# A Toeplitz convolution whose moving columns lie 4 bytes apart in place of 8, inside an attention kernel

## The chip, the cores and the metric

One core of one Trainium2 chip. The metric is the device time of one execution in microseconds (us). Each kernel was run several times; "ratio" is the mean time of a kernel's fast runs over the mean of the fast runs of the kernel before in the same rounds on the same chip, so it is not quite the ratio of the medians that stand beside it. Runs flagged slow (over 1.5% above the fastest of the same kernel) are left out of ratios. TensorE's mean granted clock is listed with each run, as a share of full speed.

## The reference, cut to what matters

Two branches over the same input `x` (2048 x 448), mixed by a gate:

```python
g = _sigmoid((x * gate_w).sum(-1, keepdims=True))
a = _A_ref(x, A_wq, A_wk, A_wv, A_wo)       # 16 heads of 28, one shared key/value head, softmax over 2048
b = _B_ref(x, B_A_re, B_A_im, ...)          # S4: K[d,l] = Re sum_n C P^l B, then a causal convolution of x with K
return g * a + (1 - g) * b
```

## The kernel before

Attention and the S4 branch are interleaved on the same engines. A list scheduler inside the program orders the operations of all engines before anything runs. It works from a cost in nanoseconds for every operation (the number after `mm` in `pg.op`), so that number changes the order of instructions and nothing else.

Attention: QK matmuls (1024) fill PSUM (the memory that TensorE writes to), an exponential on ScalarE (ACT, 410 instructions, half of them over 1536 columns and half over 1024) reads it, PV matmuls (1024, four column tiles at a time) use the result.

```python
pg.op("pe", mm, 215, ..., mode="r32")                                   # QK  (line 967)
pg.op("act", lambda e: e.activation(expT.v(...), self.psS.v(...), AF.Exp, scale=SQ), ...)   # exp (line 977)
pg.op("pe", mm, 225, mode="c32", ...)                                   # PV  (line 985)
```

S4: VectorE (DVE) builds tables of powers, TensorE turns 16 channels of them at a time into the convolution kernel K (line 792), DVE copies it into a staging tile, a DMA writes it to a scratch in HBM (the chip's main memory), and loads fetch it back as a Toeplitz matrix T: 128 partitions that each read the same scratch, shifted by one step. Four channels share a scratch row, interleaved, so the columns of one channel lie four bf16 elements, 8 bytes, apart.

```python
# scratch write: runs of 256 elements = 64 steps x 4 channels
pg.dma([(dram(self.KP, 16 * c * KPW, [[4 * KPW, 4], [256, 32], [1, 256]]),
         self.kstg.v(0, P, ks * 256, [[1, 256]]))], (128, 512), ...)

def tload(self, gi):                      # one 1 MB load for 4 channels
    pg.dma([(self.T.v(0, P, s * 4096, [[1, 4096]]),
             dram(self.KP, 4 * gi * KPW, [[4, 64], [4096, 2], [1, 4096]]))], (128, 8192), ...)

# conv (line 853): 28 chunks x 4 loads x 8 steps = 896 groups of four matmuls, one channel per column tile
for j in range(4):
    r = e.matmul(ps.v(32 * j, 33 - m, po + 128 * k, [[1, 128]]),
                 self.U.v(0, P, (m - 1) * D + 4 * gi + j, [[D, 33 - m]]),
                 self.T.v(0, P, s * 4096 + (960 - 64 * m) * 4 + j, [[4, 128]]),     # moving, step 4 elements
                 start=(m == 1), stop=(m == 15), tile_position=(0, 32 * j), ...)
...
pg.op("pe", mm, 112, rd=[("T", s), "U"], ...)                                       # told cost: 112 ns a group
```

## Time and profile before

| | before |
|---|---|
| time, median of 3 runs | 537.78 us (537.64 to 539.54) |
| span of the profiled run | 537.2 us |
| mean granted TensorE clock | 0.921 |
| conv matmuls, busy time on PE | 157.9 us |
| PE waiting for an exponential before QK (matmuls) | 27.2 us |
| last exponential ends / end of span | 519.5 / 537.2 us |

The prediction below shows most of the lines (in them PE is TensorE's matmuls and PEld its weight loads). The group line of the page gives busy us and the mean ns of one instruction, then the engine's idle time just before them.

### The profile page before, as it was taken

The numbers are of one execution on the slowest core, as the hardware profiler recorded it, in microseconds if no ns is written. First come the engines' busy times: TensorE is split into PE (matmuls) and PEld (weight loads), VectorE is DVE, ScalarE is ACT, GpSimd is POOL, SyncE is SP. The second block draws the span as 40 slices with busy tenths as digits, with TensorE's granted clock in tenths as the row PEclk, the third lists the DMA queues.
The fourth block names the chain that finished last, engine by engine and source line by source line (L and its number), as shares of the span: only waits on it lengthen the run. The fifth ranks groups of instructions, "written<-read, shape, count | busy, mean of one in ns | idle before, by whom it ended". The sixth has DMA issues, their size and how long they took to land.

```text
span 537.2 us, 18418 instructions
## 1 busy us (share of the span) xinstructions
PE 484.8 (90%) x8229; PEld 243.8 (45%) x8229; DVE 483.9 (90%) x1168; ACT 487.5 (91%) x428; POOL 4.9 (1%) x17
## 2 busy tenths in 40 slices
PE   6778888999999899999999999999999998998893
PEld 5411132553545444554545445554455543544452
DVE  4978899998999999999999999999999999999023
ACT  4599998998999999999999999999999999999960
POOL 3000000000000000000000000000000000000000
PEclk9855566997999999999999999999999999889997
DMA  8735445777798867779898896778877796697954
GB/s 232 145 79 137 138 139 207 245 285 299 249 327 297 303 230 237 253 265 345 304 337 320 262 332 238 242 260 319 309 296 267 285 393 220 176 388 254 350 188 137
DMA packets 42266, 138.16 MB, mean 257 GB/s; under 512 B 8168, under 2 KB 24476, under 8 KB 27852
## 3 DMA queue, kind: packets, MB, share of 16 engines
q1 hardware_dynamic: 40396, 135.71, 73.7%
q10 hardware_dynamic: 1792, 1.29, 0.8%
q8 instruction: 64, 1.05, 0.8%
q14 instruction: 14, 0.11, 0.1%
HBM read 133.01 MB, written 3.85 MB: 255 GB/s over the span
## 4 chain that ended last, share of the span: by engine, by line
PE 47%; ACT 36%; DVE 12%; DMA 2%; issue 1%; POOL 1%; DVEq 0%; POOLq 0%
ACT expT L977 35%; PE psS L967 13%; PE psS L853 12%; PE psB L985 8%; PE psX L792 6%; PE psX L676 2%; DMA T<-KP_scratch 2%; DVE tab L767 2%; DVE tmp L762 2%; DVE tab L759 2%; PE psS L504 1%; PE psX L877 1%; PE psX L831 1%; DVE O L883 1%; DVE tab L776 1%
## 5 line engine op out<-in xcount | busy, mean ns | idle before, releaser
L977 ACT ACTIVATE expT<-psS 128x1536 bf16<-128x1536 f32 (+1 forms) x410 | 470.8, 1254 | 19.0 <-PE psB L985 12.9
L967 PE MATMUL psS<-qT,kT 29*128 29x512 bf16 x1024 | 170.6, 412 | 29.6 <-ACT expT L977 27.2
L853 PE MATMUL psS<-T,U 128*26 128x128 bf16 (+7 forms) x3584 | 157.9, 303 | 0.6 <-DMA T<-KP_scratch 0.5
L853 PEld LDWEIGHTS psS<-T,U 128*26 128x26 bf16 (+7 forms) x3584 | 113.9, 152 | 35.3 <-issue 28.2
L985 PE MATMUL psB<-expT,vaug 128*32 128x512 bf16 x1024 | 108.8, 417 | 1.4 <-ACT gtok L643 1.3
L967 PEld LDWEIGHTS psS<-qT,kT 29*128 29x128 bf16 x1024 | 39.6, 92 | 124.4 <-ACT expT L977 92.8
L762 DVE TENSOR_TENSOR tmp<-tab,mbf 128x2048 bf16<-128x2048 bf16 (+4 forms) x140 | 78.0, 563 | 0.0
L759 DVE TENSOR_TENSOR tab<-tab,mbf 128x2048 bf16<-128x2048 bf16 (+4 forms) x140 | 77.9, 563 | 0.0
L767 DVE TENSOR_TENSOR tab<-tab,tmp 128x2048 bf16<-128x2048 bf16 (+4 forms) x140 | 77.8, 563 | 0.0
L792 PE MATMUL psX<-tab 128*32 128x96 bf16 x1792 | 54.8, 268 | 1.3 <-issue 1.2
L985 PEld LDWEIGHTS psB<-expT,vaug 128*32 128x32 bf16 x1024 | 26.6, 95 | 64.2 <-issue 60.8
L792 PEld LDWEIGHTS psX<-tab 128*32 128x32 bf16 x1792 | 41.2, 116 | 14.2 <-issue 9.0
L776 DVE TENSOR_TENSOR tab<-tab,mbf 128x2048 bf16<-128x2048 bf16 x28 | 34.0, 1216 | 0.0
L778 DVE TENSOR_TENSOR tab<-tab,mbf 128x2048 bf16<-128x2048 bf16 x28 | 34.0, 1213 | 0.0
L861 DVE TENSOR_TENSOR cst<-psS,omq 128x512 bf16<-128x512 f32 x28 | 19.0, 680 | 15.7 <-PE psS L853 15.5
L717 DVE TENSOR_TENSOR msq<-mst 128x256 f32<-128x256 f32 x63 | 26.2, 416 | 0.0
L676 PE MATMUL psX<-xT,Wq 112*128 112x512 bf16 x64 | 21.7, 436 | 0.4 <-DVE O L838 0.2
L727 DVE CAST mbf<-mst 128x256 bf16<-128x256 f32 x70 | 20.1, 288 | 0.1
L720 DVE TENSOR_TENSOR mst<-msq 128x128 f32<-128x128 f32 x70 | 19.7, 282 | 0.0
L723 DVE SCALAR_TENSOR_TENSOR mst<-mst 128x128 f32<-128x128 f32 x63 | 17.8, 283 | 0.0
L804 DVE TENSOR_REDUCE kstg<-psX 128x128 bf16<-128x256 f32 x28 | 11.7, 418 | 4.2 <-PE psX L792 4.1
L730 DVE TENSOR_SCALAR mbf<-mst 128x128 bf16<-128x128 f32 x70 | 15.3, 218 | 0.0
(112 smaller groups left out, 255.8 us busy)
## 6 DMA issues: line engine op xcount, KB each, us to landing
T<-KP_scratch SPq DMA_DIRECT2D x112, 1024.0 KB, 7.8
rdenB<-R_scratch SPq DMA_DIRECT2D x60, 64.0 KB, 3.8
U<-in_A_x_dram SPq DMA_DIRECT2D x3, 896.0 KB, 5.4
tab<-in_A_x_dram SPq DMA_DIRECT2D x4, 448.0 KB, 6.9
O<-Z_scratch SPq DMA_DIRECT2D x1, 1792.0 KB, 13.6
KP_scratch<-kstg SPq DMA_DIRECT2D x28, 64.0 KB
xT<-in_A_x_dram SPq DMA_DIRECT2D x1, 1792.0 KB, 9.2
U<-Z_scratch SPq DMA_DIRECT2D x1, 896.0 KB, 8.0
```

Source lines behind the costliest of these rows:

```text
L676: pg.op("pe", lambda e, T=T: e.matmul(px, self.Wq.v(0, DT, T * 512 + g * 128, [[1, 128]]), self.xT.v(0, DT, T * S + 512 * qc, [[1, 512]]), ...
L717: pg.op("dve", lambda e, k=k: e.tensor_tensor(msq.v(0, P, 0, [[1, 2 * BW]]) if k > 1 else msq.v(0, P, 0, [[BW, 2], [1, BW]]), src_both(k - ...
L759: pg.op("dve", lambda e, d=dst, a=src, ra=ra, w=w: e.tensor_tensor(d, a, mbf.v(0, P, ra, [[8, 16], [0, 2 * w], [1, 4]]), ALU.mult), el(n, ...
L762: pg.op("dve", lambda e, a=src, rb=rb, w=w: e.tensor_tensor(tmp.v(0, P, so, [[4 * w, 32], [1, 4 * w]]), a, mbf.v(0, P, rb, [[4, 32], [0, w ...
L767: pg.op("dve", lambda e, d=dst, t=t2: e.tensor_tensor(d, d, t, ALU.add), el(n, 1.92), rd=[("tmp", s), ("tab", s, lv + 1)], wr=[("tab", s, ...
L776: pg.op("dve", lambda e: e.tensor_tensor(ua, src, mbf.v(0, P, ra, [[8, 8], [0, 64], [1, 4]]), ALU.mult), el(2048, 1.92), rd=rk + mk, wr=[( ...
L778: pg.op("dve", lambda e: e.tensor_tensor(ub, src, mbf.v(0, P, rb, [[4, 16], [0, 32], [1, 4]]), ALU.mult), el(2048, 1.92), rd=rk + mk, wr=[ ...
L792: r = e.matmul(self.psX.v(32 * g, 32, 96 * jj, [[1, 96]]), tab.v(0, P, o + 768, [[4, 32]]), tab.v(0, P, o, [[256, 3], [4, 32]]), start=(co ...
L853: r = e.matmul(ps.v(32 * j, 33 - m, po + 128 * k, [[1, 128]]), self.U.v(0, P, (m - 1) * D + 4 * gi + j, [[D, 33 - m]]), self.T.v(0, P, s * ...
L967: r = e.matmul(self.psS.v(0, P, 1536 * s + 512 * k, [[1, 512]]), kT.v(32 * h, DH + 1, 128 * kt, [[1, 128]]), qT.v(32 * h, DH + 1, 512 * qs ...
L977: pg.op("act", lambda e: e.activation(expT.v(0, P, 512 * (i0 % 10), [[1, n]]), self.psS.v(0, P, 1536 * s, [[1, n]]), AF.Exp, scale=SQ), 75 ...
L985: r = e.matmul(self.psB.v(32 * h, 32, 0, [[1, 512]]), vaug.v(0, P, 32 * kt, [[1, 32]]), expT.v(0, P, 512 * ((4 * st + h) % 10), [[1, 512]] ...
```

## The change

The intent: halve the step of conv's moving operand, because conv takes about 0.94 ns a column in the trace before, and PV's matmuls, with a contiguous operand, 0.41 (both estimates from the lengths of bursts, which the prediction works out). The scratch and T are therefore interleaved over 2 channels, in two halves, and the scheduler is told 80 ns a group in place of 112. The arithmetic stays.

```diff
-            return e.tensor_reduce(self.kstg.v(0, P, ks * 256, [[4, 32], [1, 4]]), ...
+            return e.tensor_reduce(self.kstg.v(0, P, ks * 256, [[2, 32], [128, 2], [1, 2]]), ...
 ... (the second staging copy in the same way)
-        pg.dma([(dram(self.KP, 16 * c * KPW, [[4 * KPW, 4], [256, 32], [1, 256]]),
-                 self.kstg.v(0, P, ks * 256, [[1, 256]]))],
-               (128, 512), f"kw{ks}", ...
+        pg.dma([(dram(self.KP, (16 * c + 2 * k1) * KPW, [[4 * KPW, 4], [128, 32], [1, 128]]),
+                 self.kstg.v(0, P, ks * 256 + 128 * k1, [[1, 128]])) for k1 in range(2)],
+               (256, 256), f"kw{ks}", ...
-        pg.dma([(self.T.v(0, P, s * 4096, [[1, 4096]]),
-                 dram(self.KP, 4 * gi * KPW, [[4, 64], [4096, 2], [1, 4096]]))],
-               (128, 8192), f"T{s}", ...
+        pg.dma([(self.T.v(0, P, s * 4096 + 2048 * k1, [[1, 2048]]),
+                 dram(self.KP, (4 * gi + 2 * k1) * KPW, [[2, 64], [2048, 2], [1, 2048]])) for k1 in range(2)],
+               (256, 4096), f"T{s}", ...
-                                     self.T.v(0, P, s * 4096 + (960 - 64 * m) * 4 + j, [[4, 128]]),
+                                     self.T.v(0, P, s * 4096 + j // 2 * 2048 + (960 - 64 * m) * 2 + j % 2, [[2, 128]]),
-                pg.op("pe", mm, 112, ...
+                pg.op("pe", mm, 80, ...
 ... (the padding write of the scratch in the same way)
```

More of the change, by code (lines that the diff above doesn't have):

```diff
@@ L447, in loads @@
                 for r in range(4)], (448, 896), "wo", wr=["Wo"])
-        pg.dma([(dram(self.KP, 4 * S, [[4 * KPW, 112], [1, 256]]), self.kstg.v(0, 112, 0, [[1, 256]])),
+        pg.dma([(dram(self.KP, 2 * S, [[4 * KPW, 112], [2 * KPW, 2], [1, 128]]), self.kstg.v(0, 112, 0, [[128, 2], [1, 128]])),
                 (dram(self.Z, 0, [[256, 4], [1, 256]]), self.kstg.v(0, 4, 0, [[1, 256]]))],
@@ L803, in upper @@
             with self.nc.allow_low_precision(reason="two float32 terms, added in float32 and rounded once"):
-                return e.tensor_reduce(self.kstg.v(0, P, ks * 256, [[4, 32], [1, 4]]),
+                return e.tensor_reduce(self.kstg.v(0, P, ks * 256, [[2, 32], [128, 2], [1, 2]]),
                                        self.psX.v(0, P, 0, [[1, 32], [96, 4], [32, 2]]), AX.X, ALU.add)
         pg.op("dve", upper, el(256), rd=[X], wr=[("kst", ks)], pr=2)
-        pg.op("dve", lambda e: e.tensor_copy(self.kstg.v(0, P, ks * 256 + 128, [[4, 32], [1, 4]]),
+        pg.op("dve", lambda e: e.tensor_copy(self.kstg.v(0, P, ks * 256 + 64, [[2, 32], [128, 2], [1, 2]]),
                                              self.psX.v(0, P, 64, [[1, 32], [96, 4]])),
               el(128), rd=[X], wr=[("kst2", ks)], pr=2, unlock="X")
-        pg.dma([(dram(self.KP, 16 * c * KPW, [[4 * KPW, 4], [256, 32], [1, 256]]),
-                 self.kstg.v(0, P, ks * 256, [[1, 256]]))],
-               (128, 512), f"kw{ks}", rd=[("kst", ks), ("kst2", ks)], wr=[("KP", c)], pr=0)
+        pg.dma([(dram(self.KP, (16 * c + 2 * k1) * KPW, [[4 * KPW, 4], [128, 32], [1, 128]]),
+                 self.kstg.v(0, P, ks * 256 + 128 * k1, [[1, 128]])) for k1 in range(2)],
+               (256, 256), f"kw{ks}", rd=[("kst", ks), ("kst2", ks)], wr=[("KP", c)], pr=0)
     def tload(self, gi):
@@ L817, in tload @@
         c = gi // 4
-        pg.dma([(self.T.v(0, P, s * 4096, [[1, 4096]]),
-                 dram(self.KP, 4 * gi * KPW, [[4, 64], [4096, 2], [1, 4096]]))],
-               (128, 8192), f"T{s}", rd=[("KP", c), "pad"], wr=[("T", s)], pr=1, ns=3300)
+        pg.dma([(self.T.v(0, P, s * 4096 + 2048 * k1, [[1, 2048]]),
+                 dram(self.KP, (4 * gi + 2 * k1) * KPW, [[2, 64], [2048, 2], [1, 2048]])) for k1 in range(2)],
+               (256, 4096), f"T{s}", rd=[("KP", c), "pad"], wr=[("T", s)], pr=1, ns=3300)
     def ytr(self, c):
@@ L858, in conv @@
                 first = k == 0 and m == 1
-                pg.op("pe", mm, 112, rd=[("T", s), "U"], wr=[X, ("cst", cs)] + ([("b", 5)] if c == 0 else []) if first else [X], pr=2.5,
+                pg.op("pe", mm, 80, rd=[("T", s), "U"], wr=[X, ("cst", cs)] + ([("b", 5)] if c == 0 else []) if first else [X], pr=2.5,
                       lock="C" if first else None, slack=(2500 if gi else 9000) if m == 1 else 0, mode="c32")
```

## The prediction

> **What bounds the kernel now.** I read the page's busy shares first, then the clock slices, the windows, the waits and last the timeline of single bursts.
>
> ```profile
> PE 484.8 (90%) x8229; PEld 243.8 (45%) x8229; DVE 483.9 (90%) x1168; ACT 487.5 (91%) x428; POOL 4.9 (1%) x17
> ...
> PEclk9855566997999999999999999999999999889997
> ...
> q1 hardware_dynamic: 40396, 135.71, 73.7%
> ```
>
> Three engines are level at 90%, so no one of them alone is the bound; the windows show where each is full (columns: PE, PEld, DVE, ACT, POOL busy, then clock, DMA share, GB/s).
>
> ```profile
> 90.00:440.00 350.00, 335.29 (x6230) 174.94 (x6228) 344.19 (x855) 338.86 (x296) 0.63 (x2) 0.98 0.81 285
> 440.00:480.00 40.00, 36.81 (x673) 18.69 (x671) 38.54 (x77) 37.26 (x33) 0.00 (x0) 0.91 0.74 262
> 480.00:520.00 40.00, 35.39 (x654) 18.47 (x643) 19.12 (x36) 39.40 (x36) 0.00 (x0) 1.00 0.85 301
> ```
>
> From 90 to 440 us DVE is 98% busy and ACT 97%. From 480 DVE has little left and ACT runs at 98% to the last exponential, which ends at 520. What follows 520 is a tail of 17 us. ACT is thus the pacemaker; the reader should look for the few us in which it waits:
>
> ```profile
> PEld psS L967 <- ACT expT L977: 92.8, 231, 1.9
> ...
> ACT expT L977 <- PE psB L985: 12.9, 27, 1.4
> ...
> ACT expT L977 <- PE psS L967: 4.4, 10, 0.7
> ...
> PEld psS L853 <- DMA T<-KP_scratch: 0.8, 1, 0.8
> ```
>
> PE waits 93 us for ACT, so its 90% is inflated by pipelined latencies; it has slack. ACT waits for PE only 17.3 us, in 37 places, always short. Conv (L853) almost never waits for its data. The change makes conv on PE cheaper. Its prize is therefore the part of those 17.3 us that conv bursts cause, not conv's whole time.
>
> The costs of conv and of its comparisons:
>
> ```profile
> L977 ACT ACTIVATE expT<-psS 128x1536 bf16<-128x1536 f32 (+1 forms) x410 | 470.8, 1254 | 19.0 <-PE psB L985 12.9
> ...
> L853 PE MATMUL psS<-T,U 128*26 128x128 bf16 (+7 forms) x3584 | 157.9, 303 | 0.6 <-DMA T<-KP_scratch 0.5
> ...
> L792 PE MATMUL psX<-tab 128*32 128x96 bf16 x1792 | 54.8, 268 | 1.3 <-issue 1.2
> ...
> T<-KP_scratch SPq DMA_DIRECT2D x112, 1024.0 KB, 7.8
> ```
>
> ```profile
> 195.00 1.26 PE L792 MATMUL psX<-tab 128*32 128x96 bf16 x48
> ...
> 198.91 0.69 PE L853 MATMUL psS<-T,U 128*24 128x128 bf16 x16
> ...
> 283.49 0.73 PE L792 MATMUL psX<-tab 128*32 128x96 bf16 x24
> ...
> 300.61 0.40 PE L985 MATMUL psB<-expT,vaug 128*32 128x512 bf16 x4
> ...
> 301.48 1.16 PE L853 MATMUL psS<-T,U 128*32 128x128 bf16 x32
> ...
> 304.13 0.45 PE L831 MATMUL psX<-ident,cst 128*64 128x64 bf16 x16
> ...
> 313.16 0.61 PE L985 MATMUL psB<-expT,vaug 128*32 128x512 bf16 x8
> ```
>
> The slope between bursts gives the period of a group of four column tiles. Conv: (1.16 - 0.69) us for 4 more groups is 0.12 us for 128 columns, 0.94 ns a column. The kernel generation L792, whose moving operand also steps 8 bytes: (1.26 - 0.73) for 6 groups is 0.088 us for 96 columns, 0.92 ns. L985, contiguous: 0.21 us for 512 columns, 0.41 ns. Single records say the same: conv groups inside one burst start 120 to 122 ns apart, whether the weight load has 30 columns or 18. So weight loads do not set conv's period. A moving step of 8 bytes costs about 2.2 times a contiguous one. L831, whose moving identity steps 4 bytes, with two tiles at a time: (0.45 - 0.20 for one matmul's latency) / 7 = 0.036 us for 64 columns, 0.56 ns with all issue overhead in it. So 4 bytes looks almost like contiguous.
>
> [...] its half-clock stretches last 3.4 us or about a multiple of it, and the clock reads 0.50 between 40 and 60 us, where conv has not begun. [...]
>
> **The change, part by part.**
> Conv: 3584 / 4 = 896 groups. If 4-byte steps run at the contiguous rate, a group takes 128 x 0.41 = 53 ns plus some 12 to 15 ns for issuing four pairs (L985's group over 512 columns at full clock), so about 67 ns. Removed from PE: 896 x (121 - 67) = 48 us of streaming. The changed cost the schedule is told is 80 in place of 112; if that is nearer the truth, 896 x 35 = 31 us.
> T loads: 112 become 224 issues, of 4096-byte rows. In the trace an 8192-byte packet takes 309 ns, a 2048-byte one 84 at its fast end, so 0.0366 ns a byte plus 9 ns: 4096 bytes come to 159 ns, against 154.5 for half a long one. The loads occupy 325 us of the 16 engines' time now, so +3% is 10 us spread over the span, on queues 74% busy: hidden. SP issues 140 more at 0.52 us each: its 148 us of issuing become 221 of 537, also hidden, though a tile lands some 0.5 us later.
> The scratch writes (28, now 256-byte runs) and DVE's two PSUM copies (418 and 277 ns) keep their element counts; I take them as unchanged.
> ACT's gain: I went through every gap in ACT after 90 us and counted conv groups begun within 1 us before it ended. In 29 gaps there are some, 11 us of gap in all. Crediting each with the smaller of its length and 54 ns a group gives 5.5 us. Each removed gap also lets the next exponential overlap the one before (1254 ns mean alone, 1120 per step in the unbroken run at the end), 29 x 0.13 x one half = 2 us. Sum 7.5 us; the tail, which still has 56 conv matmuls between its steps, gives some 0.5 us.
> What comes off again is the clock. Streaming work per us of span is now: QK and PV (410 + 256) x 0.21 / 486 us = 0.29; conv 0.25; kernel generation 0.09; projections, output, transposes 0.07: together 0.70, at clock 1.0. Without conv, before 90 us, it is about 0.4 and the clock is 0.5 to 0.67. By windows of 3.4 us the fall to half clock comes below about 0.47 (an estimate from this trace). After the change the mean is 0.59, so perhaps one window in ten falls, a dozen in place of four. The gaps of 1.43, 0.79 and 0.98 us at 129, 461 and 471 us are all in or beside such windows; with less work in each I charge 0.4 us, net about +2 us.
> Sum: 538 - 8 + 2 = 532; with a little for a schedule that packs PE's queue better by the new cost, 531.
>
> **The rivals.**
> A: the clock takes it all. For: the threshold lies near the new mean[...]. Against: work per window recovers by itself as PE slows. Time 534 to 540.
> B: DVE is the bound. For: 98% from 90 to 440 us, untouched by the change. Against: it has 31 us idle after 480, so it can be up to 9 us behind ACT without setting the end. It caps the gain: not below about 522.
> C: the step is not what costs, conv stays near 120 ns a group. [...] Against: L985 and L831. Time 536 to 539.
> D: transfers become the bound (more descriptors, later tiles, 0.85 DMA share after 480). Against: 159 against 154.5 ns, and 0.8 us of waiting for T in all. Time 540 or more.
> E: the full prize, all conv-made gaps and their overlap vanish: 11 + 3 us, about 524.
>
> **Range and chances.** E and B bound it below, A and C above: 524 to 537.5. Two per cent faster is 527.0, which needs nearly all of the gaps and no loss by clock: 0.24. Slower than 548.5 needs D or a much worse static order: 0.03. Within 2%: 0.73.
>
> **What would show it.** L853's bursts: slope near 0.065 to 0.09 us a group (wrong if 0.12: C). PE's busy time falls by 30 us or more, while PEld's wait for ACT grows from 93 us. ACT's wait for L985 falls from 12.9 to about 7. The clock falls from 0.92 to about 0.89; more half-clock slices than in the middle now. DMA packets of 4096 bytes near 160 ns, T landing near 8 us, conv's DMA wait still under 3 us. The sum fails if ACT's gaps stay with conv twice as fast (then the queue order or DVE made them), or if conv's DMA waits grow to several us.

Passages that no trace or run of this case shows are cut from the recorded text where the marks stand: most of one paragraph (what is left of it tells of the half-clock stretches in the trace of the kernel before) and one reason each for the rivals A and C. No term of the sum is cut: 538 - 8 + 2 = 532, and 531 with the better packed queue. Of the step from windows to clock the traces show this much: every change of the clock, in the traces of both kernels, lies on a grid of 3.413 us, and the clock is 1.0 or 0.5. The half-clock stretches of the kernel before that end inside the span last 47.79, 6.83, 10.24, 6.83, 3.41 and 3.41 us. The 0.47 is an estimate from the work in such windows, and the table near the end of this document has the counts.

## More of the kernel before

```profile
L967 PE MATMUL psS<-qT,kT 29*128 29x512 bf16 x1024 | 170.6, 412 | 29.6 <-ACT expT L977 27.2
```

The reader is to see a mean of 412 ns for a QK matmul. Its operands do not change with the edit, and its records take 384 ns in the median at full clock and 602 at half (counted over the single records of the trace), so a change of this mean speaks of the clock.

## The result, and the profile after

The changed kernel took 552.83 us in the median of 4 runs (550.55 to 553.87) against 537.71 for the kernel before in the same rounds: ratio 1.027, with a 95% interval of 1.0229 to 1.0311. It is slower, and outside the predicted range. The granted clock was 0.83 to 0.84, against 0.92 before.

The page of the changed kernel: busy shares, the clock in 40 slices, the queue of the T loads, and four groups.

```profile
PE 471.7 (86%) x8214; PEld 227.7 (41%) x8229; DVE 484.0 (88%) x1168; ACT 488.7 (89%) x428; POOL 5.0 (1%) x17
...
PEclk9855567976999569999979989999899878998567
...
q1 hardware_dynamic: 60332, 135.72, 73.6%
...
L977 ACT ACTIVATE expT<-psS 128x1536 bf16<-128x1536 f32 (+1 forms) x410 | 471.9, 1255 | 29.5 <-PE psB L985 15.3
L967 PE MATMUL psS<-qT,kT 29*128 29x512 bf16 x1024 | 184.1, 445 | 51.6 <-ACT expT L977 47.3
...
L853 PE MATMUL psS<-T,U 128*32 128x128 bf16 (+7 forms) x3584 | 116.9, 254 | 2.5 <-issue 1.5
...
T<-KP_scratch SPq DMA_DIRECT2D x224, 512.0 KB, 6.0
```

Conv did become cheaper: 116.9 us in place of 157.9. The transfers did not move: queue share 73.6% (73.7% before), and no wait for a T load stands in the list of waits. The exponentials take the same time each. But the untouched QK matmuls grew from 412 to 445 ns in the mean (their medians are 384 ns at full clock and 602 at half, as before), and the clock row has 5s, 6s and 7s where the row before has 9s. PE's busy time fell by only 13 us (484.8 to 471.7), since QK gave back 13.5 and PV, at the lower clock, another 9.

The list of waits of the changed kernel (us in total, times, the longest):

```profile
PEld psS L967 <- ACT expT L977: 108.5, 205, 1.9
PE psS L967 <- ACT expT L977: 47.3, 109, 1.7
...
ACT expT L977 <- PE psB L985: 15.3, 21, 1.6
ACT expT L977 <- PE psS L967: 12.2, 25, 1.2
```

PE waits longer for ACT than before (108.5 and 47.3 us, was 92.8 and 27.2), and ACT at the same time waits longer for PE (27.5 us in all, was 17.3). The windows show how both can be: the kernel now has two kinds of stretches. Columns: PE, PEld, DVE, ACT and POOL busy us, granted clock, DMA share, GB/s. First the three windows of the prediction, then three chosen around one drop of the clock:

```profile
90.00:440.00 350.00, 312.96 (x6083) 157.68 (x6095) 335.82 (x838) 331.69 (x290) 0.76 (x2) 0.90 0.80 274
440.00:480.00 40.00, 35.70 (x601) 15.95 (x598) 38.55 (x73) 37.72 (x34) 0.00 (x0) 0.87 0.71 245
480.00:520.00 40.00, 34.85 (x650) 16.81 (x652) 26.66 (x54) 37.88 (x33) 0.00 (x0) 0.79 0.89 308
...
160.00:179.00 19.00, 16.16 (x342) 8.63 (x336) 19.00 (x58) 18.89 (x18) 0.00 (x0) 1.00 0.87 306
179.00:203.00 24.00, 23.53 (x280) 8.66 (x282) 19.86 (x46) 19.46 (x17) 0.00 (x0) 0.50 0.73 250
203.00:240.00 37.00, 34.47 (x732) 18.58 (x724) 35.98 (x75) 35.96 (x32) 0.00 (x0) 1.00 0.81 274
```

The same 24 us in the kernel before:

```profile
179.00:203.00 24.00, 22.50 (x339) 10.12 (x335) 24.00 (x49) 23.71 (x22) 0.00 (x0) 1.00 0.80 281
```

From 160 to 179 us ACT and DVE are full and PE is at 85%: PE has slack, as the prediction said. From 179 to 203 the clock is 0.50 for 24 us, PE is 98% busy and ACT only 81%: the bound has changed hands, and 17 ACT instructions fall into it where 22 do in the kernel before. At half clock the slack is gone; that the slack itself made the clock fall is what the experiments have to show.

The timeline of bursts (start, us, what) tells conv's cost at each clock. At full clock:

```profile
247.66 0.43 PE L853 MATMUL psS<-T,U 128*24 128x128 bf16 x16
...
250.94 0.76 PE L853 MATMUL psS<-T,U 128*32 128x128 bf16 x32
```

At half clock:

```profile
185.22 0.64 PE L853 MATMUL psS<-T,U 128*30 128x128 bf16 x16
...
187.37 0.62 PE L985 MATMUL psB<-expT,vaug 128*32 128x512 bf16 x4
...
188.46 1.89 PE L676 MATMUL psX<-xT,Wq 112*128 112x512 bf16 x4
...
190.27 0.61 PE L967 MATMUL psS<-qT,kT 29*128 29x512 bf16 x3
```

Four more groups in (0.76 - 0.43) us are 0.08 us each; by single records consecutive groups of a burst start 66 ns apart at the 25th percentile (78 in the median, which mixes both clocks). Before it was 0.12 us. A PV step takes 0.62 us where it takes 0.40 at full clock. Split by the clock, the records give 65 ns a quick conv group at full clock (25th percentile; 74 in the median) and 107 at half. Groups with an 8-byte step did not slow down: conv of the kernel before took 123 ns at full and 125 at half clock in the median, and the kernel generation of the changed kernel 91 and 92.

I sorted all exponentials after 94 us by the clock at their start, from the single records of the trace (a count over the records, not a line of a view):

| after 94 us, to the last exponential | before | after |
|---|---|---|
| full clock: us, exponentials, us per exponential | 411.6, 351, 1.173 | 330.9, 287, 1.153 |
| half clock: us, exponentials, us per exponential | 13.9, 8, 1.737 | 106.2, 73, 1.455 |
| ACT idle at full / half clock | 2.5% / 20.7% | 1.4% / 17.6% |
| last exponential ends, us | 519.5 | 531.1 |

At full clock the change does what it was made for: 0.020 us less per exponential, 287 x 0.020 = 5.7 us. At half clock 73 exponentials cost 1.455 - 1.173 = 0.282 us more each, 20.6 us; the kernel before lost 8 x 0.564 = 4.5 us that way. Net 16.1 - 5.7 = 10.4 us of the 11.6 by which the last exponential is later. The tail after it is 19.7 us in place of 17.7, with 9.5 us of it at half clock in place of 6.1. Together that is the span's 13.6 us.

### The profile page after: what moved, and what is told of

It is laid out like the page before. It is cut to its first block, busy times and chain, and to the rows that moved or that the text cites. A ratio compares the mean times of both kernels' runs of the same rounds, so it can differ in the third digit from the quotient of the medians.

```text
span 550.8 us, 18544 instructions
## 1 busy us (share of the span) xinstructions
PE 471.7 (86%) x8214; PEld 227.7 (41%) x8229; DVE 484.0 (88%) x1168; ACT 488.7 (89%) x428; POOL 5.0 (1%) x17
## 3 DMA queue, kind: packets, MB, share of 16 engines
q1 hardware_dynamic: 60332, 135.72, 73.6%
## 4 chain that ended last, share of the span: by engine, by line
DVE 38%; PE 32%; ACT 27%; issue 1%; POOL 1%; POOLq 0%
ACT expT L977 26%; PE psS L967 10%; PE psB L985 6%; DVE tmp L762 6%; DVE tab L767 6%; DVE tab L759 6%; PE psS L853 5%; PE psX L792 4%; DVE tab L776 3%; DVE tab L778 3%; PE psX L676 2%; DVE cst L861 2%; DVE O L883 1%; DVE msq L717 1%; PE psS L504 1%; DVE kstg L804 1%
## 5 line engine op out<-in xcount | busy, mean ns | idle before, releaser
L977 ACT ACTIVATE expT<-psS 128x1536 bf16<-128x1536 f32 (+1 forms) x410 | 471.9, 1255 | 29.5 <-PE psB L985 15.3
L967 PE MATMUL psS<-qT,kT 29*128 29x512 bf16 x1024 | 184.1, 445 | 51.6 <-ACT expT L977 47.3
L985 PE MATMUL psB<-expT,vaug 128*32 128x512 bf16 x1024 | 118.2, 452 | 1.6 <-ACT gtok L643 1.4
L853 PE MATMUL psS<-T,U 128*32 128x128 bf16 (+7 forms) x3584 | 116.9, 254 | 2.5 <-issue 1.5
L853 PEld LDWEIGHTS psS<-T,U 128*32 128x32 bf16 (+7 forms) x3584 | 95.2, 159 | 36.8 <-issue 32.4
L967 PEld LDWEIGHTS psS<-qT,kT 29*128 29x128 bf16 x1024 | 40.2, 93 | 137.9 <-ACT expT L977 108.5
L762 DVE TENSOR_TENSOR tmp<-tab,mbf 128x128 bf16<-128x128 bf16 (+4 forms) x140 | 78.1, 565 | 0.0
L767 DVE TENSOR_TENSOR tab<-tab,tmp 128x128 bf16<-128x128 bf16 (+4 forms) x140 | 77.6, 565 | 0.1
L985 PEld LDWEIGHTS psB<-expT,vaug 128*32 128x32 bf16 x1024 | 27.1, 96 | 73.7 <-issue 69.5
L676 PE MATMUL psX<-xT,Wq 112*128 112x512 bf16 x64 | 24.3, 474 | 0.1
L723 DVE SCALAR_TENSOR_TENSOR mst<-mst 128x128 f32<-128x128 f32 x63 | 17.9, 284 | 0.0
L681 DVE TENSOR_REDUCE absq<-psX 128x512 bf16<-128x512 f32 x16 | 11.0, 686 | 7.8 <-PE psX L676 7.8
```

The source lines that it names most:

```text
L676: pg.op("pe", lambda e, T=T: e.matmul(px, self.Wq.v(0, DT, T * 512 + g * 128, [[1, 128]]), self.xT.v(0, DT, T * S + 512 * qc, [[1, 512]]), ...
L762: pg.op("dve", lambda e, a=src, rb=rb, w=w: e.tensor_tensor(tmp.v(0, P, so, [[4 * w, 32], [1, 4 * w]]), a, mbf.v(0, P, rb, [[4, 32], [0, w ...
L767: pg.op("dve", lambda e, d=dst, t=t2: e.tensor_tensor(d, d, t, ALU.add), el(n, 1.92), rd=[("tmp", s), ("tab", s, lv + 1)], wr=[("tab", s, ...
L967: r = e.matmul(self.psS.v(0, P, 1536 * s + 512 * k, [[1, 512]]), kT.v(32 * h, DH + 1, 128 * kt, [[1, 128]]), qT.v(32 * h, DH + 1, 512 * qs ...
L977: pg.op("act", lambda e: e.activation(expT.v(0, P, 512 * (i0 % 10), [[1, n]]), self.psS.v(0, P, 1536 * s, [[1, n]]), AF.Exp, scale=SQ), 75 ...
L985: r = e.matmul(self.psB.v(32 * h, 32, 0, [[1, 512]]), vaug.v(0, P, 32 * kt, [[1, 32]]), expT.v(0, P, 512 * ((4 * st + h) % 10), [[1, 512]] ...
```

## The experiments

Three causes were open. (The expectations, which are printed as they were recorded but for one marked cut, call them K, O and D; their K2 is K and O together.) **Theory A**: the quicker conv streams less per us, the clock falls, and PE at half clock cannot keep ACT fed. **Rival B**: the static order that the scheduler makes from the told cost of 80 ns is worse. **Rival C**: the data layout (more transfers, the staging copies) costs.

### One part at a time

`e1_wide_step` is the changed kernel whose conv reads T with the old 8-byte step. The order, the data and the transfers are those of the changed kernel; the result is wrong (relative error 0.123).

```diff
-                                     self.T.v(0, P, s * 4096 + j // 2 * 2048 + (960 - 64 * m) * 2 + j % 2, [[2, 128]]),
+                                     self.T.v(0, P, s * 4096 + (960 - 64 * m) * 4 + j, [[4, 128]]),
```

> The changed kernel, only the moving operand of conv steps 8 bytes again (it reads the wrong columns, so the result is wrong on purpose); layout, transfers and static order are those of the changed kernel. Theory K (the clock: quicker conv leaves too little work per window, the clock halves, and PE makes ACT wait): conv groups back at about 120 ns, mean clock back at 0.90 to 0.93 and the time at 535 to 541 us. Rival O (the static order that the schedule builds from the smaller cost is the worse one) and rival D (transfers in twice as many pieces): 548 us or more, whatever the clock.

`e2_order_only` is the kernel before, told 80 in place of 112:

```diff
-                pg.op("pe", mm, 112, ...
+                pg.op("pe", mm, 80, ...
```

> The kernel before, only the cost told to the schedule for a conv group is 80 in place of 112; data and transfers as before. Theory K: the work per window is as before, so clock 0.90 to 0.93 and 534 to 542 us. Rival O: 548 to 555 us with a clock near 0.92. Rival D: as K.

`e5_old_order` is the changed kernel told 112, with the scheduler charged for its transfers as before, so that PE and ACT get exactly the order of the kernel before. `e16_old_order_again` is the same program, run later with more rounds.

```diff
-                free[e] = r + 450.0 * o.ndma
+                free[e] = r + 450.0 * (1 if o.slot[0] == "T" or o.slot[:2] == "kw" else o.ndma)
-               (256, 256), f"kw{ks}", rd=[("kst", ks), ("kst2", ks)], wr=[("KP", c)], pr=0)
+               (128, 512), f"kw{ks}", rd=[("kst", ks), ("kst2", ks)], wr=[("KP", c)], pr=0)
-                pg.op("pe", mm, 80, ...
+                pg.op("pe", mm, 112, ...
```

> The changed kernel with the static order of the kernel before on PE and ACT (the schedule is told the old costs), so only conv is quicker and transfers are in twice as many pieces. Theory K: the clock falls as in the changed kernel, 0.82 to 0.88, and the time is 545 to 555 us. Rival O: 530 to 538 us. Rival D: 548 to 555 us, with waits of PE for T loads of more than 5 us.

> The changed data and quick conv in the old order once more, on the chip of the two kernels with useless work, as its four runs scattered from 543.9 to 554.7: 546 to 552 us, clock 0.83 to 0.86, the runs with the lower clock the longer ones.

`e6_old_order_wide` is `e5_old_order` with the moving line of `e1_wide_step`: old order, old step, new data and transfers (wrong again).

> The previous kernel with the old order, only conv's moving operand steps 8 bytes (wrong result on purpose): layout and transfers of the change, order and conv pace of before. Theory K2 (two causes that add up: the new order costs 8 us, the quicker conv some 8 to 10 us through the clock; layout and transfers cost nothing): 536 to 541 us at a clock of 0.91 to 0.93, so 8 us or more under the same kernel with the 4-byte step (549.1). Rival D (transfers): 545 us or more.

Measured, as ratio to the kernel before in the same rounds with the 95% interval, the median, and the clock of the profiled run:

| | old order (told 112) | new order (told 80) |
|---|---|---|
| 8-byte step, old data | kernel before: 1 | e2: 1.0161 (1.0122 to 1.0200), 548.09 us, clock 0.919 |
| 8-byte step, new data | e6: 1.0031 (1.0001 to 1.0060), 538.68 us, clock 0.924 | e1: 1.0134 (1.0104 to 1.0164), 547.13 us, clock 0.914 |
| 4-byte step, new data | e5: 1.0144 (1.0087 to 1.0202), 549.12 us, clock 0.839; e16: 1.0077 (1.0031 to 1.0124), 545.07 us, clock 0.860 | changed kernel: 1.0270 (1.0229 to 1.0311), 552.83 us, clock 0.836 |

Three things follow. Rival C falls: `e6_old_order_wide` has all the new data and transfers and costs 0.3% (0.6% at the far end of its interval). Rival B is right for a part: the order alone costs 1.0 to 1.6% with the old step. The 1.0% is e1 against e6, with the changed kernel's own order; the 1.6% is e2, whose transfers are charged in one piece, so that by the traces its PE order is a third one, neither that of the kernel before nor that of the changed kernel. And the step alone costs as much again: 1.3% in the new order (1.0270 against 1.0134, intervals apart), 0.5 to 1.1% in the old one, where e5's interval is clear of e6's and e16's overlaps it. In this table the clock is at 0.84 to 0.86 wherever the step is 4 bytes, and only there.

The waits of ACT for PE show how the order works. First `e2_order_only`, then `e6_old_order_wide`:

```profile
ACT expT L977 <- PE psB L985: 14.3, 31, 1.1
ACT expT L977 <- PE psS L967: 8.6, 19, 1.3
```

```profile
ACT expT L977 <- PE psB L985: 11.3, 27, 1.1
ACT expT L977 <- PE psS L967: 5.2, 10, 0.9
```

In the order of e2 ACT waits 22.9 us for PE (22.9 in e1 too, 14.5 and 8.4), in the old one 16.5, at the same conv speed and the same clock. In e2 the full-clock pace is 1.189 us per exponential over 351 of them, against 1.173 before: 5.6 of the 7.8 us by which its last exponential is later (527.3 against 519.5).

For the step in one order, here is the cleanest pair: the windows of `e5_old_order`, then of `e6_old_order_wide`, which differ in conv's moving operand only.

```profile
94.00:450.00 356.00, 321.09 (x6239) 163.44 (x6242) 345.02 (x853) 341.51 (x298) 0.63 (x2) 0.92 0.83 283
450.00:520.00 70.00, 62.98 (x1111) 29.29 (x1104) 50.61 (x100) 65.02 (x57) 0.00 (x0) 0.74 0.80 273
```

```profile
94.00:450.00 356.00, 337.91 (x6319) 177.27 (x6319) 351.67 (x864) 346.79 (x303) 0.63 (x2) 0.99 0.83 288
450.00:520.00 70.00, 62.55 (x1182) 33.19 (x1181) 48.01 (x97) 66.78 (x59) 0.00 (x0) 0.98 0.79 274
```

Less work on PE, a clock of 0.92 and 0.74 in place of 0.99 and 0.98, and 355 ACT instructions in the two windows in place of 362, with the DMA share the same. By the records, e5 spent 100.1 us at half clock (70 exponentials, 1.431 us each) and e6 12.5 us; at full clock e5's pace was 1.157 against 1.175. So 70 x (1.431 - 1.175) = 17.9 us lost, 289 x 0.018 = 5.2 gained, 2.0 that e6 loses at half clock itself: 10.7 us, where the last exponential is 9.6 later. (e16, with 76.8 us at half clock, comes out between them.)

Inside one program the clock also goes with the time. The same e5 ran at clock 0.872 in 543.87 us, at 0.851 in 549.07, at 0.839 in 549.18 and at 0.828 in 554.65 (flagged slow). Over the fast runs alone of the seven programs with a 4-byte step and no added instruction (the changed kernel, e5, e12 and e16 to e19, 31 runs), each compared only with runs of the same program, 1 us more at half clock goes with 0.24 us more time (standard error 0.03), not far from the 20.6 / 106.2 = 0.19 of the account above. That is a correlation; it does not say which of the two moves the other.

### Is the told cost right, and does it matter that it is?

`e12_told_66` tells the changed kernel the true cost of a group (80 becomes 66), `e13_before_told_121` tells the kernel before its true cost (112 becomes 121).

> The changed kernel, only the schedule is told 66 ns for a conv group, which is its measured period at full clock, in place of 80. If the new order was bad because the told cost was wrong: 545 to 550 us. If orders scatter by some 8 us whatever is told: anywhere in 543 to 560, with the clock at 0.82 to 0.86.

> The kernel before, told 121 ns, its measured period, in place of 112. If a truer cost gives a better order: 530 to 537 us. If orders scatter: 536 to 550 us at a clock of 0.91 to 0.93; the 112 of the kernel before would then be a picked winner.

e12: 1.0202 (1.0124 to 1.0280), clock 0.837; the ratio rests on two fast runs of 545.38 and 553.16 us, since the other two were flagged slow (the median of all four is 554.75). e13: 1.0000 (0.9963 to 1.0038), 538.25 us, with another order on PE than before. A truthful number does not by itself give a better order: 112, 121 and 80 for a group of 121 ns gave 1.000, 1.000 and 1.016; 112, 80 and 66 for a group of about 67 ns gave 1.008 to 1.014, 1.027 and 1.020. Why 80 makes a worse order I have not found out.

### Giving the clock its work back by adding instructions

If too little streaming is the cause, more streaming should bring the clock back. Six kernels tried it with instructions that do no useful work.

`e4_twice` issues every conv matmul twice in the changed kernel and halves the result in a factor used later (right):

```diff
-                    for j in range(4):
+                    for i, j in ((i, j) for i in range(2) for j in range(4)):
-                                     start=(m == 1), stop=(m == 15), ...
+                                     start=(m == 1 and i == 0), stop=(m == 15 and i == 1), ...
```

> The changed kernel with every conv matmul issued twice and the factor behind it halved, so the result is right; a group then takes about 2 x 66 = 132 ns, somewhat over the 121 of before. Theory K: the clock comes back to 0.91 or more and the time to 536 to 543 us although PE does more work than in the changed kernel. Rivals O and D: no gain, 552 us or more, as work is only added.

It took 610.03 us (1.1281), 57 us over the changed kernel: about all that the added groups stream (896 x 66 ns = 59 us), as if PE had had no slack, and with a clock of 0.89 to 0.90 in the fast runs (0.876 in the profiled one, which was among the slow ones, so its numbers here tell only what sort of wait it has). A wait in it and a piece of its timeline:

```profile
PE psS L853 <- issue: 26.1, 23, 2.6
```

```profile
152.31 1.29 PE L853 MATMUL psS<-T,U 128*32 128x128 bf16 x55
155.45 0.34 PE L853 MATMUL psS<-T,U 128*20 128x128 bf16 x9 [1.84 <-issue]
```

PE stands still for 1.84 us inside a burst, waiting for no semaphore. The records hold 26 such stalls over 0.3 us, 32.4 us in all; 24 of them end 1.0 to 1.7 us after a packet of 16 KB has landed on an instruction queue (92 such packets in all; the kernel before has 64, and 1.2 us of such stalls). That PE had run out of instructions is my estimate from this timing; it was not shown, since no experiment moved these packets alone.

`e7_filler` adds groups to `e5_old_order` that the real conv overwrites later, clustered in the first of the four loads of a chunk:

```diff
+                    n = 384 - 128 * k
+                    if k == 0 or (k == 1 and m % 4 == 1):
+                        for j in range(4):
+                            r = e.matmul(ps.v(32 * j, 33 - m, po + 512 - n, [[1, n]]), ..., start=True, stop=True, ...)
```

> Old order, quick conv, and twelve useless groups of matmuls a chunk (384 or 256 contiguous columns, into columns of the bank that are overwritten later; right result), which give PE back some 52 us of streaming. Theory K2: the clock returns to 0.89 to 0.93 and the time falls below 544, to 536 to 543 us, though PE has more to do. If the clock were only a companion of the slowdown and not its cause: 549 us or more.

It took 566.39 us (1.0546) at clock 0.92, and it came out wrong (relative error 0.067). e14 and e15, without the start flag and over zeros, come out right, but no run changed the flag alone, so the cause was not shown.

`e14_zero_full` and `e15_zero_half` add groups over a tile of zeros, without a start flag, spread over the chunk (16 and 9 groups; both right):

```diff
+                    if m in ((5, 13), (3, 7, 11), (1, 5, 9, 13), (1, 3, 5, 7, 9, 11, 13))[k]:      # e15: ((7,), (7, 13), (3, 11), (3, 7, 11))
+                        n = 512 - 128 * k
+                        for j in range(4):
+                            r = e.matmul(ps.v(32 * j, 33 - m, po + 128 * k, [[1, n]]), ...,
+                                         self.zt.v(0, P, 0, [[0, n // 64], [1, 64]]), start=False, stop=False, ...)
```

> Old order, quick conv with the 4-byte step, and after some conv groups a group of useless matmuls with a moving operand of zeros (2, 3, 4 and 7 of them for the four tiles of a chunk, 512 to 128 columns wide, right result), spread as evenly as conv itself: about 1.7 us a chunk or 48 us in all, what the 8-byte step had cost. Theory K2 (the time is lost because the clock halves, and it halves because PE streams too little): clock 0.90 to 0.93 and 536 to 543 us, below the same kernel without the useless work. If the step of the operand matters in another way: 549 us or more.

> The same with half of the useless work, some 23 us. Theory K2: clock 0.87 to 0.91; if the load's cost and the clock's gain balance somewhere between, this is the best of the three, 533 to 543 us, perhaps under the kernel before. Otherwise between 540 and 549.

e14: 1.0437 by its two fast runs (559.86 and 565.38 us, clock 0.928 and 0.911; the other four were flagged slow, and the median of all is 571.54), 15.5 us of stalls without a semaphore. e15: 1.0109 by its three fast runs (543.48 to 546.06 us, clock 0.902 to 0.920; the median of all six is 550.43), 10.0 us of such stalls. Both profiled runs, from which the stalls come, were slow ones. The clock came back in step with the dose; the time did not.

`e10_pv_half_twice` and `e11_pv_all_twice` issue the PV matmuls of `e5_old_order` a second time, over their first 256 or all 512 columns (the denominators double with the sums, so the results are right):

```diff
+                for h in range(4):
+                    r = e.matmul(self.psB.v(32 * h, 32, 0, [[1, 256]]), vaug.v(0, P, 32 * kt, [[1, 32]]),
+                                 expT.v(0, P, 512 * ((4 * st + h) % 10), [[1, 256]]), start=False, ...)     # e11: 512
```

> Old order, quick conv, and each PV matmul issued a second time over the first 256 of its 512 columns (numerator and denominator of those columns both double, so the result is right): 256 x 0.12 us = 31 us of streaming more, placed behind the step that ACT waits for rather than in it. Theory K2 (the clock is the cause): fewer half-clock windows, clock 0.87 to 0.91, and the time falls below the 549.1 of the same kernel without them, to 537 to 546 us, although only work is added. If added load costs what it did in the kernels with QK twice (0.26 to 0.77 us per us): 557 us or more.

> The same with all 512 columns twice: 58 us of streaming more. Theory K2: clock 0.91 or more; time 540 to 555 us, as the load by then costs as much as the clock gives. Rival (load is all): 565 us or more.

e10: 547.99 us (1.0193), clock 0.904 to 0.927, 6.0 us of stalls. e11: 552.86 us (1.0269), clock 0.926 to 0.940. Again clock bought, time not.

### The two steps at the same clock

`e8_before_qk_twice` and `e9_fast_qk_twice` issue the QK matmuls twice in the kernel before and in `e5_old_order`:

```diff
-                for k, (qc, g, kt, h) in enumerate(ts):
+                for k, (qc, g, kt, h) in list(enumerate(ts)) * 2:
```

> The kernel before with each QK matmul issued twice (second one overwrites the first with the same values; right result): 410 x 0.21 = 86 us of streaming more, everywhere, also before conv begins. If PE's pace matters through its load: 545 to 560 us. If the clock outweighs load, above all in the half-clock stretch up to 94 us: 532 to 539 us, clock 0.97 or more.

> Old order, quick conv, each QK matmul twice (right result). Theory K2: clock 0.96 or more and 530 to 542 us, clearly under the same kernel without the second QK (549.1). Rival (PE's load is what costs): 555 us or more.

e8: 603.57 us (1.1227), clock 0.936. e9: 571.15 us (1.0612), clock 0.929. With PE loaded enough to hold the clock in both, the quick conv is 32 us faster; without the doubling it is 6 to 10 us slower in the same order (e16 and e5 against the kernel before of their rounds). The exponentials' lines of e8 and of e9:

```profile
L977 ACT ACTIVATE expT<-psS 128x1536 bf16<-128x1536 f32 (+1 forms) x410 | 482.1, 1239 | 71.1 <-PE psS L967 34.3
```

```profile
L977 ACT ACTIVATE expT<-psS 128x1536 bf16<-128x1536 f32 (+1 forms) x410 | 477.8, 1244 | 43.8 <-PE psS L967 16.8
```

ACT's idle time falls from 71.1 to 43.8 us. So a cheaper conv does pay where PE is loaded. The comparison is not pure: the doubling also moves the bound towards PE. From 94 to 450 us PE is 98% busy and ACT 87% in e8, where in e6 they are 95% and 97%.

### The dose without added instructions

To free the test from the stalls, three kernels leave the instruction count of `e5_old_order` alone and let a conv matmul stream its columns more than once, in place of a slower read (results right, since the last pass stands in the right columns and later tiles overwrite the rest):

```diff
-                        r = e.matmul(ps.v(32 * j, 33 - m, po + 128 * k, [[1, 128]]),
+                        w = (3, 2, 2, 1)[k]                 # e18: (2, 1, 2, 1), e19: (1, 2, 1, 1)
+                        r = e.matmul(ps.v(32 * j, 33 - m, po + 128 * k, [[1, 128 * w]]),
-                                     self.T.v(..., [[2, 128]]),
+                                     self.T.v(..., [[0, w], [2, 128]]),
```

> Old order, quick conv, no instruction added: each conv matmul streams its 128 columns three times for the first tile of a chunk, twice for the next two, once for the last; the copies fall into columns that are overwritten later, so the result is right. Mean group 119 ns at full clock, what the 8-byte step had. Theory K2: with the same PE occupancy[...], the clock is 0.91 to 0.93 and the time 536 to 542 us, below the 545 to 549 of the same kernel without the copies. If the 4-byte step costs in another way than the clock: 548 us or more.

> The same with the copies at the first and third tile only, once each: mean group 92 ns, about half of the useless work. Theory K2: clock 0.88 to 0.91 and 536 to 545 us; the best of the three if the gain of the clock outweighs the load here.

> One copy at the second tile only: mean group 79 ns. Theory K2: clock 0.86 to 0.89, 540 to 548 us, between the half dose and no copies.

| | extra columns | ratio | median us | clock | us at half clock after 94 us |
|---|---|---|---|---|---|
| e5 / e16 | none | 1.0144 / 1.0077 | 549.12 / 545.07 | 0.839 / 0.860 | 100.1 / 76.8 |
| e19 | a quarter more | 1.0165 (1.0111 to 1.0218) | 549.66 | 0.880 | 55.6 |
| e18 | half more | 1.0095 (1.0047 to 1.0144) | 544.04 | 0.906 | 30.3 |
| e17 | as many again | 1.0113 (1.0071 to 1.0155) | 546.49 | 0.932 | 5.6 |
| e6, the 8-byte step | none, but a slower read | 1.0031 (1.0001 to 1.0060) | 538.68 | 0.924 | 12.5 |

The windows of `e17_longer_full`, to be held against those of e6 above:

```profile
94.00:450.00 356.00, 335.02 (x6286) 179.22 (x6296) 348.69 (x857) 343.75 (x299) 0.63 (x2) 1.00 0.83 285
450.00:520.00 70.00, 62.27 (x1160) 32.56 (x1158) 50.80 (x102) 67.01 (x60) 0.00 (x0) 0.98 0.80 274
```

That the clock follows the streaming is shown: with nothing changed but how many columns the same instructions stream, the half-clock time falls from 100 or 77 to 56, 30 and 6 us. Each of these is one profiled run, but the clocks of all fast runs go the same way: 0.839 to 0.878 for e5 and e16, then 0.860 to 0.880, 0.888 to 0.906 and 0.919 to 0.932. That the time follows the clock is not shown by this series: at e6's clock and e6's PE load, e17 has 299 ACT instructions in the first window where e6 has 303, and it is some 0.8% longer. Its full-clock pace is 1.188 us per exponential, e6's 1.175. e17's groups are uneven (up to three passes in one load of a chunk, one in another), where e6's are all 121 ns, and no run tested whether that is why. What stays open is therefore how much of the 4-byte step's loss one could win back at full clock. The range is between nothing, as these fillers show, and the some 5 us that the full-clock pace of e5 would give.

No version beat the kernel before.

## Why the prediction was wrong, by its own steps

**Conv's cost: right.** It said 67 ns a group; the records show 66 at their fast quarter. Its inference that steps of 4 bytes read almost like contiguous ones holds (its 67 was worked out from the contiguous rate); why a step of 8 bytes is slower, no run shows.

**Transfers: right.** Packets of 4096 bytes take 159 ns in the median, as said; the queue share is unchanged, no T wait. A half tile lands in 6.0 us, sooner than the 8 it named. Its rivals C and D fall.

**ACT's gain at equal clock: right in kind, somewhat too large.** It summed 7.5 to 8 us; at full clock the pace gained 5.7 us over 287 exponentials.

**PE's waits for ACT grow from 93 us: right** (108.5). **PE busy falls by 30 us or more: wrong** (13 us), and **ACT's wait for PV's step falls to about 7: wrong** (15.3), both for the reason that follows.

**The clock: this step failed.** The fall of the clock was named, its size was not. The prediction put it as "perhaps one window in ten falls, a dozen in place of four" and "with less work in each I charge 0.4 us, net about +2 us", and it dismissed its rival A because "work per window recovers by itself as PE slows". The clock went to 0.836, not 0.89. Measured: 106.2 us at half clock, 31 windows of 3.41 us in place of 4, and 20.6 us lost, 0.66 per window; net about +16.

What failed inside this step is the recovery. I laid the records from 94 to 520 us on the grid of 3.413 us on which the clock changes in these traces and charged every matmul its streaming time at full clock (66 ns for a quick conv group, 121 for a slow one, 88 for one of kernel generation, some 0.42 ns a column for the rest). The load of a window is then an estimate, as a share of the window:

| clock in a window and in the next | before: windows, load | after: windows, load |
|---|---|---|
| full, then full | 118, 0.49 to 0.87 | 87, 0.40 to 0.85 |
| full, then half | 3, 0.43 to 0.49 | 9, 0.32 to 0.48 |
| half, then half | 1, 0.46 | 20, 0.34 to 0.48 |
| half, then full | 3, 0.56 to 0.61 | 8, 0.41 to 0.60 |

The mean load of the full-clock windows is 0.70 before and 0.60 after, as the prediction summed, the falls lie about its estimate of 0.47 (not sharply: 8 of the 87 are below 0.48), and 9 of 96 windows led to a fall, its "one window in ten". But a fall lasted 3.1 windows in the mean, and 1.3 before. In the kernel before the clock was back after 3 of the 4 half-clock windows, as the prediction assumed. In the changed kernel the work did not recover by itself: in the 28 half-clock windows PE was busy 97% of the time by the profile and did only 0.45 of a window's work, and in 20 of them the clock stayed down. The same count over `e5_old_order` gives 9 falls (0.37 to 0.47), 19 windows that stayed down (up to 0.49) and 8 recoveries (from 0.51). Half clock also did not slow all of PE alike: quick conv went from 65 to 107 ns a group (at the 25th percentile), a QK matmul from 384 to 602 ns (median), and groups with an 8-byte step kept their time (123 and 125 ns for conv before, 91 and 92 for the kernel generation after).

**The order: this step failed too.** "With a little for a schedule that packs PE's queue better by the new cost" took 1 us off. The order made from 80 costs 1.0 to 1.6% at the old step, by e1 and e2. "A much worse static order" stood in the text, among the reasons for a 3% chance of slower.

By ratios, the 2.7% is 1.3% for the order with its data (e1) and 1.3% for the step in that order, at rounding. The account by clock state above cuts the same time another way: with quick conv the order's cost shows itself not in the full-clock pace (1.153 against 1.157 in e5) but in part as more time at half clock and the rest not resolved.

## What to carry to other kernels

Before making matmuls cheaper on a TensorE that is not the bound, look at how near its clock is to falling: count half-clock windows and the load in them. Here the slow operand read went with a clock of 0.924 (e6) and the quick one, in the same order, with 0.839 (e5); and from 179 to 203 us, at half clock, PE was 98% busy and ACT 81%: the engine that had slack had become the bound. Ask not only how often the clock will fall but also whether the work that the engine does at half clock is enough to lift it again (a fall lasted 3.1 windows in the mean after the change, 1.3 before). Change a cost that a static scheduler is told in a run of its own; the order it makes is a change by itself, and a truthful cost need not make a better order. When filler work is added to test such a theory, prefer longer instructions to more instructions (at the full dose 1.1% in e17 against 4.4% in e14), and expect that the filler's own cost can eat what the clock returns (e17 came to a clock of 0.932, and to 1.0113 where e5 and e16 had 1.0144 and 1.0077).
